# A transformer block's prologue: modulation and k's products ahead of q, q's folds last and in 64 by 64 tiles

## The chip, the core and the metric

The kernel runs on one core of one Trainium2 chip. The metric is the device time of one execution in microseconds. Its engines are TensorE (PE; its weight loads are listed apart as PEld), VectorE (DVE), ScalarE (ACT), GpSimd (POOL) and SyncE (SP), which here only issues transfers. Each engine works through its own list of instructions in order and waits at an instruction until what it needs is there.

## The reference

x has 2048 tokens of 640 features; there are 32 heads of 20. All data are float32.

```python
mod = (silu(c) @ w_mod).reshape(1, 6, 1, 640)
sa, ca, ga, sb, cb, gb = ...              # six rows of 640
h = layernorm(x) * (1 + ca) + sa
q, k, v = split_heads(h @ wqkv)
pq = einsum("bhsd,hdf->bhsf", q, w_phi)   # the same for pk
phi = concat([softmax(p), softmax(-p)])   # of pq and of pk
kv = einsum("bhsf,bhsd->bhfd", phi_k, v); z = phi_k.sum over tokens
o = (phi_q @ kv) / (phi_q . z + 1e-6)
x = x + ga * (o @ wo)
h = layernorm(x) * (1 + cb) + sb
x = x + gb * (relu(h @ w1 + b1)**2 @ w2 + b2)
```

## The kernel before

**Tiling.** Tokens go in 16 tiles of 128, features in 5 chunks of 128. x is loaded, normalised and transposed two token tiles at a time (a pair; pair 0 holds tiles 0 and 1). A matrix is held as a high part in a rounded format and a low part, the rest; a product is three matmuls: high by high, high by low, low by high (`three`, L87). ScalarE copies the high part, VectorE subtracts to get the low part (`lo`, L90).

**Folding.** w_phi is multiplied into the q and k columns of wqkv, so that a projection gives pq or pk at once. `fold` (L265) does this for one chunk d of 128 features: the raw columns, transposed on the host, are the stationary operand and a block-diagonal tile of w_phi (`bd_t`, six heads to a block of 120) is the moving one; five matmuls of 120 columns and one of 40 fill two PSUM tiles, each float32 matmul as two instructions. `split` then makes the high and the low part.

**Modulation.** `mod_rows2` (L568) multiplies silu(c) with one chunk of the first two modulation rows in four column groups; `mod_sb` copies the sums, `mod_cols2` transposes them and reduces them on VectorE to one column of scale and shift per chunk. `t_in` transposes normalised x, `t_out` applies that column on ScalarE (`hf`, then the high part `hT`) and VectorE subtracts the low part. `stats` takes the mean and variance of a pair on VectorE and finishes them on GpSimd; `scale` normalises in place on ScalarE.

**Order.** The prologue up to the values of tiles 0 and 1 is written out by hand: each engine does its instructions in the order in which the code writes them. It opens with `WARM` matmuls on a tile of ones. Behind it, TensorE's order is still by hand, that of the other engines is set by the scheduler of the language from its own estimate of the times. In the prologue before, SyncE issues k, x pair 0, q (four chunks), modulation chunks 0 and 1, q's last, the other modulation chunks, x pair 1, v. TensorE folds all of k and four chunks of q, then does the modulation rows and transposes of x, and k's products (`k_step`, L603: chunk d for tiles 0 and 1, so the two tiles hold all four buffers of the `pj` PSUM tiles). Then come q, x pair 1's transposes, q of tile 1, v of tiles 0 and 1, and from there tile by tile k, v and q, with the products of phi_k and v (`do_kv`, L443, tile `kvp`) for two tiles at a time. These need the exponentials of both tiles divided by their sums (`k_norm`, L437). `spread` subtracts maximum and minimum per head, `exps` takes the exponentials.

Of the kernel before, what the change touches and what calls it, by code (L numbers as in the profile page):

```python
# [26 lines left out]
NG = len(GR)  # L27
NU = 11
# [7 lines left out]
WARM = 9  # L36
# [18 lines left out]
def kernel(  # L55
# [8 lines left out]
    bd: bass.AP,  # L64
    c: bass.AP,
# [98 lines left out]
    make_identity(nc, ident)  # L164
    neg = const.tile([P, P], F32R, name="neg")
# [36 lines left out]
    nc.scalar.dma_start(c_t, c)  # L202
    bd_t = row("s4", "bd_t")
    raw, WM, RV, XB = {}, {}, {}, {}

    def load_raw(nm, w5, w1, ds=range(NC)):
        if 0 in ds:
            raw[nm] = [tok2("w", f"raw_{nm}{i}") for i in range(3)]
            nc.vector.memset(raw[nm][2][:, 1], 0.0)
        for d in ds:  # L210
            nc.sync.dma_start(raw[nm][d // 2][:, d % 2], w5[d * P : (d + 1) * P])
            if d == 0:
                nc.sync.dma_start(raw[nm][2][:40, 1], w1)
# [5 lines left out]
    def load_wm(d):  # L219
        WM[d] = flat(tok2(("k", "k", "q0", "q1", "w")[d], f"wm_{d}"))  # L220
        nc.sync.dma_start(WM[d], w_ss[d * P : (d + 1) * P])
# [4 lines left out]
    load_raw("k", wk5, wk1)  # L226
    load_x(0)
    load_raw("q", wq5, wq1, range(4))
    for d in range(2):
        load_wm(d)  # L230
    load_raw("q", wq5, wq1, (4,))
    for d in range(2, NC):
        load_wm(d)
    load_x(1)
    for d in range(NC):
# [3 lines left out]
        nc.sync.dma_start(RV[d], wv[d * P : (d + 1) * P])  # L239
# [25 lines left out]
    def fold(nm, d, p=None):  # L265
# [4 lines left out]
        for g, (o, n) in enumerate(GR):  # L270
            if g < 5:
                r = raw[nm][d // 2][:120, d % 2, g * P : (g + 1) * P]
            else:
                r = raw[nm][2][:120, 1, d * P : (d + 1) * P]
            nc.tensor.matmul(  # L275
                p[g // 3][:, (g % 3) * 120 : (g % 3) * 120 + n], r, bd_t[:120, g * 120 : g * 120 + n],
                start=True, stop=True,
            )

        def split():  # L280
            for h, (a, b) in enumerate(((0, 360), (360, 640))):
# [261 lines left out]
    def stats(xt, nm):  # L543
# [5 lines left out]
        for i in range(2):  # L549
            for h in range(2):  # L550
                nc.vector.bn_stats(st[:, i, h], xt[:, i, h * HALF : (h + 1) * HALF])
            nc.vector.bn_aggr(mv[:, i], st[:, i])
        nc.gpsimd.tensor_scalar(sq, mv[:, :, 1], EPS, None, op0=ALU.add)
# [3 lines left out]
        return nb, sq  # L557
# [10 lines left out]
    def mod_rows2(*ds):  # L568

        p = tp(f"mrow{ds[0]}")  # L570
        for m, d in enumerate(ds):
# [45 lines left out]
    for d in range(4):  # L617
        fold("k", d)()
# [1170 lines left out]
```

## Time and profile before

| | us |
|---|---|
| median of 3 runs (lowest, highest) | 747.8 (746.73, 747.94) |
| the profiled execution | 746.64 |
| its span, first to last instruction | 744.9 |
| TensorE / VectorE / ScalarE / GpSimd busy | 738.1 / 598.8 / 453.1 / 169.1 |

The profiled execution takes 1.74 us outside its span. A row of a timeline gives the start, the duration, the engine, the line of the kernel, the operation, out<-in, the shape and the count of instructions merged into it, and in brackets the idle time before them with what ended it. Times are from the start of the span. In a row of the chain of waits the line is that of a helper where one records the matmul (L81). TensorE's ends are modelled, its starts are recorded. A row of a table of windows gives the stretch, its length, and each engine's busy time with its count of instructions, then TensorE's granted clock, the share of busy transfer engines and GB/s.

### The profile page before, as it was taken

To read this page: it belongs to the slowest core of one execution; us is meant where nothing else is said; L and a number is where in the kernel's file an instruction comes from. 1 tells how busy PE (TensorE), PEld (TensorE's weight loads), DVE (VectorE), ACT (ScalarE), POOL (GpSimd) and SP (SyncE) were. 2 spreads that over 40 slices of the span, in tenths; PEclk is the share of its full clock that TensorE was granted. 3 is DMA by queue.
4 is the path that set the end of the run, shared out by engine and by line. 5 is a ranking of instruction groups with operands and counts; after the bars stand their busy time and mean duration, and the time that the engine had idled before them with its cause. 6 is when DMAs were issued, how large, how long until landed. Compare 5 with 4: busy or idle time off the path is not lost.

```text
span 744.9 us, 16612 instructions
## 1 busy us (share of the span) xinstructions
PE 738.1 (99%) x6523; PEld 720.6 (97%) x6523; DVE 598.8 (80%) x1089; ACT 453.1 (61%) x1028; POOL 169.1 (23%) x352
## 2 busy tenths in 40 slices
PE   9999999999999999999999999999999999999997
PEld 9999999999999988998999999999999999999997
DVE  6598988987999999999755777877786776777766
ACT  5767566657863355567687667475574747647431
POOL 2000101001100337547303040231321313222110
PEclk9999999999999999999999999999999999999999
DMA  8812341343331254754885567897667768667461
GB/s 330 339 37 106 111 134 59 107 143 107 126 124 72 83 184 152 173 137 106 209 251 166 154 199 255 271 312 211 180 190 201 214 184 240 187 176 213 129 183 36
DMA packets 58800, 126.46 MB, mean 170 GB/s; under 512 B 7438, under 2 KB 16403, under 8 KB 58723
## 3 DMA queue, kind: packets, MB, share of 16 engines
q1 hardware_dynamic: 38636, 79.20, 32.4%
q0 software_dynamic: 17504, 40.90, 22.1%
q10 hardware_dynamic: 2583, 5.30, 1.9%
q8 instruction: 51, 0.84, 0.5%
q14 instruction: 26, 0.21, 0.1%
HBM read 100.74 MB, written 29.89 MB: 175 GB/s over the span
## 4 chain that ended last, share of the span: by engine, by line
PE 88%; DVE 6%; ACT 3%; POOL 1%; issue 1%; ACTq 0%; DVEq 0%; POOLq 0%
PE up L81 25%; PE acc L81 18%; PE pk L81 8%; PE pwo L81 8%; PE pv L81 8%; PE pq L81 6%; PE acc3x L81 5%; PE te L943 2%; PE kvp L448 1%; DVE dn L875 1%; PE foldk L275 1%; PE numa L81 1%; PE ta L357 1%; DVE scr L873 1%; PE foldq L275 1%
## 5 line engine op out<-in xcount | busy, mean ns | idle before, releaser
L81 PE MATMUL up<-h,w 128*128 128x256 f32 x1640 | 204.6, 276 | 0.1
L81 PEld LDWEIGHTS up<-h,w 128*128 128x128 f32 x1640 | 196.5, 188 | 0.7 <-DVE h L91 0.5
L1338 ACT ACTIVATE ft<-up,b_t 128x256 f32<-128x256 f32 x104 | 49.2, 473 | 95.6 <-PE up L81 95.2
L81 PE MATMUL acc<-w,ra 128*128 128x384 f32 x452 | 97.5, 335 | 0.0
L1339 DVE TENSOR_TENSOR ft<-ft 128x256 f32<-128x256 f32 x104 | 43.8, 421 | 43.0 <-ACT ft L1338 41.5
L81 PE MATMUL pwo<-wo,ot 128*128 128x384 f32 (+1 forms) x480 | 78.1, 313 | 0.0
L81 PE MATMUL pq<-wq,hT 128*128 128x384 f32 (+1 forms) x480 | 75.8, 312 | 0.0
L81 PEld LDWEIGHTS acc<-w,ra 128*128 128x128 f32 x452 | 72.7, 188 | 0.8 <-DVE ra L91 0.6
L81 PE MATMUL pk<-wk,hT 128*128 128x384 f32 (+1 forms) x480 | 73.1, 309 | 0.0
L81 PE MATMUL pv<-wv,hT 128*128 128x380 f32 (+1 forms) x480 | 73.0, 309 | 0.0
L81 PEld LDWEIGHTS pwo<-wo,ot 128*128 128x128 f32 x480 | 69.5, 188 | 2.8 <-issue 2.7
L81 PEld LDWEIGHTS pq<-wq,hT 128*128 128x128 f32 x480 | 71.3, 188 | 0.7 <-issue 0.5
L81 PEld LDWEIGHTS pv<-wv,hT 128*128 128x128 f32 x480 | 71.3, 188 | 0.0
L81 PEld LDWEIGHTS pk<-wk,hT 128*128 128x128 f32 x480 | 70.8, 188 | 0.5 <-ACT hT L369 0.2
L91 DVE TENSOR_TENSOR ra<-ft,ra 128x384 fp32r<-128x384 f32 (+2 forms) x86 | 36.8, 448 | 32.6 <-ACT ra L1362 18.8
L1448 POOL DMA_DIRECT2D ring_a<-td_a x34 | 18.5, 543 | 117.2 <-PE acc L81 103.5
L1362 ACT ACTIVATE ra<-ft 128x384 fp32r<-128x384 f32 x48 | 25.2, 526 | 28.4 <-DVE ft L1339 22.3
L81 PE MATMUL acc3x<-w,ra 128*128 128x256 f32 x231 | 39.5, 278 | 0.0
L81 PEld LDWEIGHTS acc3x<-w,ra 128*128 128x128 f32 x231 | 37.2, 188 | 0.0
L439 DVE TENSOR_REDUCE sk<-ek 128x64 f32<-128x1280 f32 x16 | 23.7, 1482 | 15.1 <-ACT ek L434 10.7
L1353 DVE TENSOR_TENSOR ft<-ft 128x128 f32<-128x128 f32 x136 | 33.3, 286 | 1.2
L334 POOL TENSOR_SCALAR sma<-sma 128x2 f32<-128x2 f32 x6 | 3.1, 516 | 134.9 <-ACT xb L333 134.9
(255 smaller groups left out, 1442.5 us busy)
## 6 DMA issues: line engine op xcount, KB each, us to landing
ring_c<-td_c POOLq DMA_DIRECT2D x34, 384.0 KB, 4.0
ring_a<-td_a POOLq DMA_DIRECT2D x34, 384.0 KB, 3.4
ring_b<-td_b POOLq DMA_DIRECT2D x34, 256.0 KB, 3.6
esp<-eq SPq DMA_DIRECT2D x12, 640.0 KB
el<-esp SPq DMA_DIRECT2D x12, 640.0 KB
rw<-in_w SPq DMA_DIRECT2D x23, 320.0 KB
wm<-in_w_mod SPq DMA_DIRECT2D x20, 320.0 KB
xb<-in_x SPq DMA_DIRECT2D x8, 640.0 KB
```

The source lines that it names most:

```text
L81: nc.tensor.matmul(o, a, b, start=first and i == 0, stop=last and i == len(terms) - 1, skip_group_check=skip,)
L91: (eng or nc.vector).tensor_tensor(out_lo, full, hi.bitcast(F32), op=ALU.subtract)
L275: nc.tensor.matmul(p[g // 3][:, (g % 3) * 120 : (g % 3) * 120 + n], r, bd_t[:120, g * 120 : g * 120 + n], start=True, stop=True,)
L357: nc.tensor.transpose(p[:, i * P : (i + 1) * P], src, ident)
L439: nc.vector.tensor_reduce(s, heads(flat(e)), axis=AX.X, op=ALU.add)
L448: nc.tensor.matmul(kvp[0][32 * c : 32 * c + DH + 1, a - g % 3 * DH : a - g % 3 * DH + 2 * m].rearrange("p (s n) -> p s n", s=2)[:, :, h % ...
L943: nc.tensor.transpose(p[:124, a : a + P], EU[2 * j + i][:, 2 * g + c, :124], ident)
L1338: nc.scalar.activation(r, p, AF.Relu, bias=b1_t[:, f : f + 1])
L1339: nc.vector.tensor_tensor(r, r, r, op=ALU.mult)
L1353: nc.vector.tensor_tensor(t[:, o], t[:, a], t[:, b], op=op)
L1362: nc.scalar.activation(a[:, 0, :3], t[:, :3], AF.Copy)
L1448: nc.gpsimd.dma_start(RING[j, n, r], TD[n][r].bitcast(F32R))
```

## The change

**Loads.** SyncE issues k chunks 0 and 1, x pair 0, k chunks 2 and 3, modulation chunk 0, k chunk 4, modulation chunks 1 to 3, x pair 1, modulation chunk 4 and then q. v's loads are put after the code of the prologue's k products. A one-element copy on GpSimd from q's chunk 3 into v's first tile holds them until that chunk has landed; in SyncE's list they come behind five loads for the gate modulation, which use the memory of the five copied modulation rows.

**TensorE's order.** Only four k folds come first, then modulation chunk 0, x's transposes and k's last fold; k's products begin at once, with the transpose of the next modulation column between the two tiles of a step and the modulation rows of the one after behind it. q's folds come last, chunk 0 before k's last step, the others behind it.

**q's folds.** q's raw columns are laid out anew: heads 0 to 15 on partitions 0 to 59, heads 16 to 31 on 64 to 123. The new tile `bq_t` holds three heads to a block of 60. A group of columns is four matmuls of 64 by 64 by 60, one for each half of the rows and of the columns; the two row halves write to two PSUM tiles, which are now four fixed ones in turn (`kvp` 1 with the one of `tp`, `kvp` 2 with `kvp` 0). A chunk has 24 matmuls (48 instructions) in place of 6 (12), with half the depth.

**The rest.** Two warm matmuls less; x pair 1's statistics are split around chunk 0's q fold; k's results of tile 1 are copied behind all q copies, x pair 1's scaling after them, then v's high parts; tile 1's `spread` follows all of v's low parts.

```diff
-WARM = 9
+WARM = 7
...
+    own6 = bdc[:, 376:382]
+    own_q = own6[:, :3]
...
+    nc.scalar.dma_start(bdc[:, 256:376], bdq)
+    bq_t = row("s4", "bq_t")
...
+    for step in ("k0", "k1", "x0", "k2", "k3", "m0", "k4", "m1", "m2", "m3", "x1", "m4", "q0", "q1", "q2", "q3", "q4"):
...
+    def load_v():
+        nc.gpsimd.tensor_copy(RV[0][:1, :1], raw["q"][1][:1, 1, :1])
+        for d in range(NC):
+            nc.sync.dma_start(RV[d], wv[d * P : (d + 1) * P])
...
+        if nm == "q":
+            for g, (o, n) in enumerate(Q_FOLDS):
+                r = raw[nm][d // 2][:, d % 2, g * P : (g + 1) * P] if g < 5 else raw[nm][2][:, 1, d * P : (d + 1) * P]
+                for a in (0, 64):
+                    for c in (0, 64):
+                        nc.tensor.matmul(
+                            p[a // 64][c : c + 64, o : o + n], r[a : a + 64, c : c + 64], bq_t[a : a + 64, o : o + n],
+                            start=(g == 0), stop=True, skip_group_check=True,
+                        )
...
-    for d in range(4):
+    for d in range(2):
         fold("k", d)()
-    n0 = stats(XB[0], "a0")
-    fold("k", 4)()
-    fold("q", 0, kvp[1:])()
-    fold("q", 1)()
+    _, n0 = stats_parts(XB[0], "a0")
+    nc.vector.tensor_tensor(
+        bq_t[:, :360].rearrange("p (g i f) -> p g i f", i=3, f=DH),
...
+    for d in range(2, 4):
+        fold("k", d)()
     scale(XB[0], *n0)
-    fold("q", 2)()
-    split = fold("q", 3)
     mod_rows2(0)
     mod_sb(0)
     for d in range(NC):
         t_in(XB[0], d, TR[d])
-    split()
+    fold("k", 4)()
     mod_cols2(0)
     out0(0)
     mod_rows2(1)
     mod_sb(1)
...
+    def fold_q(d):
+        p = (kvp[2], kvp[0]) if d % 2 else (kvp[1], tp(f"foldq{d}"))
+        fold("q", d, p)()
...
+    for d in range(NC):
+        k_step(d, lambda: next_out(d + 1))
+        if d + 2 < NC:
+            mod_rows2(d + 2)
+            mod_sb(d + 2)
+        if d == 2:
+            next(n1)
+        if d == 3:
+            fold_q(0)
+            n1 = next(n1)
+    load_v()
     load_x(2)
...
+    to_sb(PP[0], PK[0])
+    for d in range(1, NC):
+        fold_q(d)
+    to_sb(PP[1], PK[1])
+    scale(XB[1], *n1)
...
-    for d in range(1, NC):
+    for d in range(NC):
         v_hi(d)
...
+    v_lo(0)
+    v_lo(1)
     spread(PK[0], EK[0], "k0")
     exps(EK[0])
-    v_lo(1)
     v_lo(2)
-    spread(PK[1], EK[1], "k1")
     v_lo(3)
     v_lo(4)
+    spread(PK[1], EK[1], "k1")
     do_q(0)
```

Three places show how it moves instructions. A row gives the line, the operation, out<-in and the shape; xN merges N alike. Line numbers of the changed kernel are its own (L305 and L295 are the folds, L609 the modulation rows, L389 x's transposes, L622 the modulation's transposes, L83 the products).

TensorE before, from the first modulation rows to k's first product:

```order
L577 MATMUL mrow0_362<-wm_0_151,cs_175 32x128 x10
L357 MATMUL kvp0_76<-ident_87,xb0_140 128x128 x2
L357 MATMUL kvp1_77<-ident_87,xb0_140 128x128 x4
L357 MATMUL kvp2_78<-ident_87,xb0_140 128x128 x4
L590 MATMUL kvp0_76<-ident_87,msb0_373 128x128
L577 MATMUL mrow1_395<-wm_1_153,cs_175 32x128 x10
L275 MATMUL foldq4_0_409<-bd_t_129,raw_q2_144 128x120 x3
L275 MATMUL foldq4_1_410<-bd_t_129,raw_q2_144 128x120 x2
L275 MATMUL foldq4_1_410<-bd_t_129,raw_q2_144 128x40
L590 MATMUL kvp0_76<-ident_87,msb1_406 128x128
L577 MATMUL mrow2_423<-wm_2_156,cs_175 32x128 x10
L81 MATMUL pk0_0_438<-wk0_235,hT0_222 128x384 x3
```

TensorE with the change, at the same place (behind k's fold 3):

```order
L305 MATMUL foldk3_1_291<-bd_t_134,raw_k2_138 128x40
L609 MATMUL kvp0_76<-wm_0_144,cs_177 32x128 x10
L389 MATMUL kvp1_77<-ident_87,xb0_155 128x128 x4
L389 MATMUL kvp2_78<-ident_87,xb0_155 128x128 x4
L389 MATMUL kvp0_76<-ident_87,xb0_155 128x128 x2
L305 MATMUL foldk4_0_327<-bd_t_134,raw_k2_138 128x120 x3
L305 MATMUL foldk4_1_328<-bd_t_134,raw_k2_138 128x120 x2
L305 MATMUL foldk4_1_328<-bd_t_134,raw_k2_138 128x40
L622 MATMUL kvp0_76<-ident_87,msb0_314 128x128
L609 MATMUL kvp0_76<-wm_1_145,cs_177 32x128 x10
L83 MATMUL pk0_0_357<-wk0_235,hT0_224 128x384 x3
```

Two modulation steps and q's chunk 4 stood between x's transposes (L357) and the first product; now x's transposes come ahead of k's last fold, and one modulation step stands before the first product.

ScalarE before, from x pair 1's scaling to v's last high part (`wv0` to `wv4` are v's high parts, `k0` and `k1` the copies of k's results of tiles 0 and 1):

```order
L561 ACTIVATE xb1_162<-xb1_162,nba1_504,sqa1_503 128x640 x2
L658 ACTIVATE wv0_565<-rawv0_164 128x640
L424 ACTIVATE k0_568<-pk0_0_438 128x384
L424 ACTIVATE k0_568<-pk0_1_439 128x256
L424 ACTIVATE k1_571<-pk1_0_440 128x384
L424 ACTIVATE k1_571<-pk1_1_441 128x256
L658 ACTIVATE wv1_574<-rawv0_164 128x640
L658 ACTIVATE wv2_576<-rawv2_167 128x640
L658 ACTIVATE wv3_578<-rawv2_167 128x640
L658 ACTIVATE wv4_580<-rawv4_170 128x640
```

ScalarE with the change, from q's last copies to the same end:

```order
L314 ACTIVATE wq4_626<-kvp1_77 128x320
L314 ACTIVATE wq4_626<-foldq4_625 128x320
L456 ACTIVATE k1_534<-pk1_0_359 128x384
L456 ACTIVATE k1_534<-pk1_1_360 128x256
L595 ACTIVATE xb1_164<-xb1_164,nba1_454,sqa1_453 128x640 x2
L705 ACTIVATE wv0_659<-rawv0_149 128x640
L705 ACTIVATE wv1_661<-rawv0_149 128x640
L705 ACTIVATE wv2_663<-rawv2_150 128x640
L705 ACTIVATE wv3_665<-rawv2_150 128x640
L705 ACTIVATE wv4_667<-rawv4_151 128x640
```

Scaling and v's first high part stood ahead of the copies of k's results; now they stand behind all of q's copies and the last of k's.

VectorE before, around the division of k tile 3 (`ek3` divided by `sk3`; behind the prologue, where the scheduler sets the order):

```order
L439 TENSOR_REDUCE sk3_1121<-ek3_1100 128x64
L91 TENSOR_TENSOR hT2_1008<-hfa2_4_1148,hT2_1008 128x256
L428 TENSOR_REDUCE mxq3_1168<-q3_1164 128x32
L429 TENSOR_REDUCE mxq3_1168<-q3_1164 128x32
L440 RECIPROCAL sk3_1121<-sk3_1121 128x64
L431 TENSOR_TENSOR eq3_1167<-q3_1164,mxq3_1168 128x640 x2
L441 TENSOR_TENSOR ek3_1100<-ek3_1100,sk3_1121 128x1280
L428 TENSOR_REDUCE mxk4_1335<-k4_1188 128x32
L429 TENSOR_REDUCE mxk4_1335<-k4_1188 128x32
L476 TENSOR_REDUCE rs_q_106<-eq3_1167 128x64
L291 SCALAR_TENSOR_TENSOR wm1280_3_1177<-wm1280_3_1177,cs_175,wm1280_2_1026 128x640
```

VectorE with the change, at the same place:

```order
L93 TENSOR_TENSOR hT2_1096<-hfa2_4_1236,hT2_1096 128x256
L460 TENSOR_REDUCE mxq3_1256<-q3_1252 128x32
L461 TENSOR_REDUCE mxq3_1256<-q3_1252 128x32
L471 TENSOR_REDUCE sk3_1209<-ek3_1188 128x64
L463 TENSOR_TENSOR eq3_1255<-q3_1252,mxq3_1256 128x640 x2
L460 TENSOR_REDUCE mxk4_1423<-k4_1276 128x32
L461 TENSOR_REDUCE mxk4_1423<-k4_1276 128x32
L472 RECIPROCAL sk3_1209<-sk3_1209 128x64
L508 TENSOR_REDUCE rs_q_110<-eq3_1255 128x64
L323 SCALAR_TENSOR_TENSOR wm1280_3_1265<-wm1280_3_1265,cs_177,wm1280_2_1114 128x640
L473 TENSOR_TENSOR ek3_1188<-ek3_1188,sk3_1209 128x1280
```

The division now follows the two reductions of `k4`, the sum `rs_q` and the modulation step `wm1280_3`, which all came after it, while `hT2` chunk 4 and q3's reductions went ahead of the sum `sk3`.

153 lines of the change are left out of this document (82 added, 71 removed).

## The prediction

> **What bounds the kernel now.** I read the page's totals first, then the chain of waits in order of time for the first 80 us, then the timeline of each engine there.
>
> ```profile
> span 744.9 us, 16612 instructions
> PE 738.1 (99%) x6523; PEld 720.6 (97%) x6523; DVE 598.8 (80%) x1089; ACT 453.1 (61%) x1028; POOL 169.1 (23%) x352
> 1.05 4.21 PE warm L616 x18
> 5.26 6.80 PE foldk L275 x60
> 12.06 1.34 PE kvp L275 x12
> 13.40 4.02 PE foldq L275 x36
> 17.41 0.78 PE mrow L577 x20
> 18.19 1.24 PE kvp L357 x10
> 24.63 0.11 PE kvp L590
> 28.32 5.20 PE pk L81 x36
> 33.52 4.31 PE pq L81 x30
> 43.22 8.81 PE pv L81 x60
> 52.03 4.34 PE pk L81 x30
> 60.77 1.41 PE kvp L448 x125
> ...
> 5.26:33.52 28.26, 28.26 (x296) 26.96 (x296) 16.61 (x46) 19.55 (x45) 3.29 (x10) 1.00 1.03 393
> ```
>
> The chain rows give start, duration, engine, result and line. TensorE carries the chain from 1.05 us on, and in the window from its first fold to q's first product (33.52) it is busy in all 28.26 us. The prologue is therefore a sum of TensorE work, with folds of both matrices (1.34 us a chunk) put where the loads, x's statistics and the modulation are being waited for. Whatever leaves TensorE there is gained; whatever makes it wait there is lost. The rest of the program follows at a TensorE that hardly ever waits, so a shift at 60 us is still there at the end. The second thing to see is VectorE behind it:
>
> ```profile
> 32.82 0.82 DVE L91 TENSOR_TENSOR wv<-rawv,wv 128x640 fp32r<-128x640 f32 x1 [1.89 <-ACT wv L658]
> 55.63 1.48 DVE L441 TENSOR_TENSOR ek<-ek,sk 128x1280 f32<-128x1280 f32 x1
> 86.38 1.49 DVE L441 TENSOR_TENSOR ek<-ek,sk 128x1280 f32<-128x1280 f32 x1
> ...
> 32.82:87.86 55.04, 50.39 (x66) 1.00 0.25 85
> ...
> 89.74 1.48 PE L448 MATMUL kvp<-ek,vt 128*21 128x40 f32 x128
> ```
>
> From v's first low part (32.82) to the division of k tile 3 (86.38, ends 87.87) it is busy 50.39 of 55.04 us. The division of tile 1 ends at 57.11, 3.7 us before the kv products that need it (60.77); that of tile 3 ends 1.9 us before its kv products (89.74). These two margins are what a late VectorE can use up.
>
> **The start.** Two warm matmuls less are worth 2 x 4.21/9 = 0.94 us of TensorE, but the first fold stands behind the block-diagonal tile as well:
>
> ```profile
> 4.25 0.85 DVE L243 TENSOR_TENSOR bd_t<-bdc 120x360 f32<-120x360 f32 x2 [1.99 <-DMA bdc<-in_bd]
> 5.05 7.00 PE L275 MATMUL foldk<-bd_t,raw_k 120*128 120x120 f32 x60
> ```
>
> Its first part is made at 4.25 to 4.78, so the fold can start 0.2 us earlier at most. I take nothing. The extra transfer of q's diagonal and the five small GpSimd instructions lie beside this and cost nothing, since what they make is first needed by an instruction behind x's statistics; late, they would cost what they are late.
>
> **The loads.** When they land is read from SyncE's issues, which wait for the transfer eight places earlier:
>
> ```profile
> 8.07 1.15 SPq L221 DMA_DIRECT2D wm<-in_w_ss  x2
> 8.89 0.33 SPq L221 DMA_DIRECT2D wm<-in_w_ss  x1
> 10.83 0.33 SPq L211 DMA_DIRECT2D raw_q<-in_wq  x1
> ...
> SPq L211 <- DMA xb<-in_x: 1.6, 1, 1.6
> SPq L221 <- DMA raw_k<-in_wk: 0.8, 2, 0.5
> ```
>
> They say that k chunk 3 had landed by 8.07, chunk 4 by 8.89, x by 10.83, which is after 1.4, 1.7 and 2.4 MB. With the same bytes in the new sequence, x lands at about 8.1, k chunk 2 at 8.9, chunk 3 at 9.9, the first modulation chunk at 11.7 (0.65 MB more at the 0.393 MB per us of the window above), k chunk 4 at 12.5. TensorE then does k's chunks 0 and 1 from 5.05 to 7.9, waits 1.0, does 2 and 3 from 8.9 to 11.6 and the first modulation rows to 12.5. q's loads land at some 21 to 25, before their use at 29. v's are queued behind five loads that wait for the last modulation transpose (28 us by the sum below); they land by 35 and are used at 39, so holding them costs nothing (of the one-element copy that holds them, GpSimd has nothing behind it until the next tiles' statistics). Without that cover ScalarE would stop there, and behind v's copies q's results with it.
>
> **From x to the first product.** Statistics come behind the low part of chunk 1 in VectorE's order:
>
> ```profile
> 6.63 0.99 DVE L91 TENSOR_TENSOR wk<-foldk,wk 128x360 fp32r<-128x360 f32 x2 [0.73 <-ACT wk L282]
> 7.97 0.99 DVE L91 TENSOR_TENSOR wk<-foldk,wk 128x360 fp32r<-128x360 f32 x2 [0.35 <-ACT wk L282]
> 11.55 0.88 DVE L551 BATCH_NORM_STATS2 sta<-xb 128x6 f32<-128x320 f32 x2
> 13.46 0.21 DVE L552 BATCH_NORM_AGGREGATE mva<-sta 128x2 f32<-128x12 f32 x1
> 15.43 1.73 ACT L561 ACTIVATE xb<-xb,nba,sqa 128x640 f32<-128x640 f32 x2 [0.25 <-POOL nba L556]
> 19.81 0.15 DVE L592 TENSOR_REDUCE cols_a<-kvp 128x2 f32<-128x4 f32 x1
> 20.60 0.42 ACT L369 ACTIVATE hT<-hfa 128x256 fp32r<-128x256 f32 x1
> ```
>
> They start at 8.96 instead of 11.55; 2.12 us later they are done (11.08), scaling starts 1.76 after that (12.84) and ends at 14.57. The ten transposes wait for it: TensorE stands 2.1 us from 12.5, transposes to 15.87, and only then has chunk 4's fold (to 17.21). Its low part ends 2.57 after the fold's start (5.05 to 7.62 for chunk 0), at 18.44, and the first modulation column is reduced behind it on VectorE. From the reduction to the transposed, modulated x took 19.81 to 21.02, so k's first product is at **19.75**: another 1.6 us of waiting, the second modulation rows (0.78) inside it. It was at 22.7. This is where I chose: all waits are charged in full since the order has nothing else for TensorE there.
>
> A step of k is 5.20/3 = 1.73, one transpose 0.11 and one set of rows 0.78 between: 2.62. That covers the path from a transpose to the next chunk (24.63 to 26.18 now). Three such steps, one of 1.84, a q fold and the last 1.73 end k's products at 19.75 + 7.86 + 1.84 + 0.85 + 1.73 = 32.0.
>
> **The q folds.** No instruction of before works on 64 by 64 tiles. Nearest are those that use a part of the columns or of the rows:
>
> ```profile
> 247.92 0.87 PE L811 MATMUL z<-kvs,ident 21*128 21x360 f32 x8
> ```
>
> z, on four row groups: 1280 columns at two half passes. A fold has 640 columns x 2 passes in 1.34 us, 1.05 ns each, so z is worth 2.7 us alone and took 0.87: 3 at a time. The kv products give the other bound, 11 ns per instruction (1.41 us for 125, of 40 columns in four column groups). A q chunk is 48 instructions of mostly 60 columns: 48 x 11 = 0.53 at the least; 320 columns x 4 x 2 x 1.05 = 2.7 us if nothing runs side by side; 0.9 at z's three. I take 0.85, next to z, which has row groups and a bank for each as the q fold has. Each fold then saves 0.49, 2.4 in all. The Trainium skill, "TensorE: Matmul & The Clock Gate", section "Wait — 56ns, not 53.3ns?", has a floor of about 25 ns from one matmul's start to the next, which would make a chunk 1.2 us and the five 1.75 us longer than in my sum. The kv row, 11 ns, does not agree with it.
>
> ```profile
> 18.51 0.76 ACT L282 ACTIVATE wq<-foldq 128x360 fp32r<-128x360 f32 x2
> 32.70 1.39 ACT L424 ACTIVATE k<-pk 128x384 f32<-128x384 f32 x4
> ```
>
> Folds 1 to 4 stand between k's and q's products with two sets of banks, where before they filled waits. Copies of a chunk take 0.76 (the like pair of q's copies), the second low part ends about 0.5 later: fold 3 waits for fold 1's low part. 32.0, 32.9, 33.7 | 34.2, 35.05 | 35.9: q's products start at **35.9**, 2.4 us later than the 33.52 of now.
>
> **VectorE behind it.** ScalarE's order has all q copies (36.7), two of k's copies (0.70, half of 1.39: 37.4), x tile pair 1's scaling (1.74: 39.1) and then v's first high part (0.7). VectorE's first low part of v starts at 39.8, not 32.82: **7.0 late**, with k's first tile ready since 32 and waiting behind it. From there it has its 50.39 us up to the division of tile 3; the order now also puts ahead of this division four instructions that came after it (k4's two reductions, a sum, a modulation step):
>
> ```profile
> 65.51 1.49 DVE L439 TENSOR_REDUCE sk<-ek 128x64 f32<-128x1280 f32 x1 [2.38 <-ACT ek L435]
> 87.78 0.81 DVE L428 TENSOR_REDUCE mxk<-k 128x32 f32<-128x640 f32 x1
> 91.42 1.55 DVE L431 TENSOR_TENSOR ek<-k,mxk 128x640 f32<-128x640 f32 x2
> ```
>
> 3.64 us (87.78 to 91.42). One wait for an exponential pair remains, 1.5 of the 2.38. 39.8 + 50.4 + 3.6 + 1.5 = 95.3, and the kv products of tiles 2 and 3 start there instead of at 89.74: **5.6 us later**. On the way, tile 1's division ends at 39.8 + 24.3 = 64.1, 3.4 later than kv's start now, so 3.4 of the 5.6 are lost by then. After it VectorE is ahead of TensorE again (the division of tile 5 now precedes its q work). Nothing behind that gives time back.
>
> The sum against the profiled execution: 746.64 + 5.6 = 752.2. That execution lies 1.2 below the median of the runs shown (747.8, within 746.73 to 747.94), so I add half of that: 752.8.
>
> **Rivals.** (1) VectorE's 1.9 us margin holds and the division of tile 3 isn't late, since part of the 50.39 can run while it waits for ScalarE: then the 3.4 us at tile 1 is all, 750.0 to 751.2. For it: VectorE has 4.65 us idle before 87.86. Against it: the four instructions put ahead of the division.
>
> (2) Faster: the path from x to k's first product overlaps more than I charge. The sum runs on from this product: q's products 16.15 later, tile 1's division 44.35 later. It decides at 16.4 us (60.77 - 44.35), provided tile 3's division is not pushed out either; below 17.4 TensorE alone would be ahead. With the first product at 15, 746.6 - 1.4 = 745.2, or 746.4 from the median. For it: the 5.1 us of waiting in my sum (1.0, 2.1, 1.6 and 0.45 between the q folds) are the whole loss, against 2.4 us of folding saved. Against it: statistics, scaling, transposes, chunk 4 and the reduction follow one another on four engines, each with its row above. Between 16.4 and 17.5 lies no change.
>
> (3) TensorE slower than its rows. Warm instructions take 4.21/18 = 0.234 us, folds 6.80/60 = 0.113: with the shorter warming and the wait at 8 us, the slow pace could reach into k's first two folds: 24 x 0.121 = 2.9 more, 755.7. The Trainium skill, "TensorE: Matmul & The Clock Gate", Part 1, has a clock that is released only after about 3.4 us of activity; by it the shorter warming can give this same 755.7 at most. The granted clock in the window above reads 1.00, and nothing in the trace shows a lower one. Or the tiles do not run side by side: 5 x 1.85 less the 0.45 of waiting that it covers, 761.6.
>
> **How the numbers follow.** Forecast 0.44; rival (1) 0.26; (3) 0.12; (2) 0.09 faster and 0.09 no change. What a measurement here can tell is about 0.2%, 1.5 us. Slower 0.82, same 0.09, faster 0.09. The forecast's own range is 750.5 to 755.5. To hold the time 8 times in 10 it reaches down over (1) to 748.0 and up over the first half of (3) to 757.0.
>
> **What would show it.** In the profile after: k's first product near 19.75, the transposes waiting for scaled x some 2 us; a q fold of 0.85 us (0.53 to 2.7); q's first product near 35.9; v's first low part near 39.8 on VectorE; TensorE waiting for VectorE before the kv products, twice. I am wrong if q's products start before 33.5 or v's first low part before 35, and wrong in the size if neither kv product waits.

## The result, and the profile after

The changed kernel takes 757.89 us (median of 4 runs, 754.19 to 758.35) against 747.87 us (746.73 to 748.56) for the kernel before on the same chip: a ratio of 1.0118, 95% interval 1.0096 to 1.0141 (the quotient of the two medians, 1.0134, lies inside it). Its profiled execution took 757.99 us.

From the page of the changed kernel, its span and totals:

```profile
span 756.0 us, 16975 instructions
PE 741.4 (98%) x6699; PEld 722.3 (96%) x6699; DVE 600.1 (79%) x1090; ACT 452.7 (60%) x1028; POOL 166.1 (22%) x357
```

The span grew by 11.1 us, TensorE's busy time by only 3.3. The rest, 7.8 us, is TensorE waiting. The chain of waits of the changed kernel shows where (start, duration, what):

```profile
5.08 4.86 PE foldk L305 x24
...
10.84 0.81 DVE sta L583 x2
...
14.79 1.74 ACT xb L595 x2
16.58 2.18 PE kvp L389 x9
18.76 1.08 PE foldk L305 x6
...
22.52 1.25 PE pk L83 x6
...
68.29 1.41 PE kvp L480 x125
```

In place of an unbroken row of TensorE work, the chain goes from k's first two folds to x's statistics on VectorE, to its scaling on ScalarE, back to TensorE for the transposes, and on to k's first product at 22.52, where it was at 22.7 before. In the kernel before, all folds of k and of q were done by then; here those of k are, and those of q are not. TensorE's timeline of the changed kernel at the places of the prediction:

```profile
15.77 0.33 PE L389 MATMUL kvp<-ident,xb 128*128 128x128 f32 x1 [2.39 <-ACT xb L595]
16.58 2.18 PE L389 MATMUL kvp<-ident,xb 128*128 128x128 f32 x9 [0.48 <-ACT xb L595]
...
37.92 1.32 PE L295 MATMUL kvp<-bq_t,raw_q 64*64 64x60 f32 x52 [0.35 <-DVE wq L93]
...
40.23 4.58 PE L83 MATMUL pq<-wq,hT 128*128 128x384 f32 x30
...
68.22 1.48 PE L480 MATMUL kvp<-ek,vt 128*21 128x40 f32 x128
...
100.71 0.84 PE L480 MATMUL kvp<-ek,vt 128*21 128x40 f32 x64 [2.62 <-DVE ek L473]
101.48 6.13 PE L83 MATMUL pq<-wq,hT 128*128 128x384 f32 x30
```

q's first product starts at 40.23 (before 33.52 in the chain and 33.36 in the timeline: 6.7 to 6.9 later), the kv products of tiles 0 and 1 (the products of phi_k and v) at 68.3 (60.8 before: 7.5 later), and between those of tile 2 and those of tile 3 TensorE stands 2.62 us for the division on VectorE. Windows of the changed kernel, at its first folds, up to q's first product, and around x's wait (the number behind GpSimd's is the granted clock):

```profile
5.00:9.00 4.00, 3.92 (x18) 3.93 (x19) 1.87 (x8) 0.93 (x3) 1.10 (x8) 1.00 1.03 368
...
5.08:40.23 35.15, 30.66 (x476) 27.86 (x476) 15.72 (x46) 16.35 (x37) 4.04 (x16) 0.95 0.76 271
...
16.00:17.00 1.00, 0.52 (x3) 0.42 (x3) 0.00 (x0) 0.78 (x2) 0.00 (x0) 0.53 1.02 394
17.00:18.00 1.00, 1.00 (x7) 1.00 (x6) 0.00 (x0) 0.00 (x0) 0.00 (x0) 0.50 1.08 420
```

From the first fold to q's first product, 4.49 of 35.15 us are idle, where the kernel before had none in 28.26; and at 17 us, behind the wait for x, the granted clock is 0.50. From 5 to 9 us it reads 1.00, yet only 18 fold instructions were done there in 3.92 us.

### The profile page after: what moved, and what is told of

Its sections match the earlier page's. It is cut to its first block, busy times and chain, and to the rows that moved or that the text cites. A ratio compares the mean times of both kernels' runs of the same rounds, so it can differ in the third digit from the quotient of the medians.

```text
span 756.0 us, 16975 instructions
## 1 busy us (share of the span) xinstructions
PE 741.4 (98%) x6699; PEld 722.3 (96%) x6699; DVE 600.1 (79%) x1090; ACT 452.7 (60%) x1028; POOL 166.1 (22%) x357
## 4 chain that ended last, share of the span: by engine, by line
PE 89%; DVE 5%; ACT 2%; DMA 1%; issue 1%; POOL 1%; SPq 0%; ACTq 0%; DVEq 0%
PE up L83 24%; PE acc L83 18%; PE pk L83 9%; PE pv L83 9%; PE pwo L83 8%; PE pq L83 7%; PE acc3x L83 5%; PE te L986 2%; PE kvp L480 1%; PE numa L83 1%; PE ta L389 1%; DMA xb<-in_x 1%; PE numb L83 1%; DVE dn L918 1%; PE foldk L305 1%
## 5 line engine op out<-in xcount | busy, mean ns | idle before, releaser
L83 PE MATMUL up<-h,w 128*128 128x256 f32 x1640 | 204.7, 276 | 0.1
L83 PEld LDWEIGHTS up<-h,w 128*128 128x128 f32 x1640 | 196.5, 188 | 0.7 <-DVE h L93 0.5
L83 PE MATMUL acc<-w,ra 128*128 128x384 f32 x452 | 97.5, 335 | 0.0
L83 PE MATMUL pwo<-wo,ot 128*128 128x384 f32 (+1 forms) x480 | 78.5, 314 | 0.0
L83 PE MATMUL pq<-wq,hT 128*128 128x384 f32 (+1 forms) x480 | 77.5, 316 | 0.0
L83 PE MATMUL pk<-wk,hT 128*128 128x384 f32 (+1 forms) x480 | 74.2, 310 | 0.2 <-ACT hT L401 0.2
L83 PEld LDWEIGHTS acc<-w,ra 128*128 128x128 f32 x452 | 72.7, 188 | 1.0 <-DVE ra L93 0.8
L83 PEld LDWEIGHTS pq<-wq,hT 128*128 128x128 f32 x480 | 72.8, 191 | 0.8 <-issue 0.5
L83 PE MATMUL pv<-wv,hT 128*128 128x380 f32 (+1 forms) x480 | 73.1, 310 | 0.3 <-ACT q L456 0.3
L83 PEld LDWEIGHTS pwo<-wo,ot 128*128 128x128 f32 x480 | 69.9, 188 | 2.8 <-issue 2.7
L83 PEld LDWEIGHTS pk<-wk,hT 128*128 128x128 f32 x480 | 71.2, 188 | 1.3 <-issue 0.6
L83 PEld LDWEIGHTS pv<-wv,hT 128*128 128x128 f32 x480 | 71.3, 188 | 0.5 <-ACT q L456 0.5
L1491 POOL DMA_DIRECT2D ring_a<-td_a x34 | 18.5, 543 | 117.1 <-PE acc L83 103.5
L83 PE MATMUL acc3x<-w,ra 128*128 128x256 f32 x231 | 39.5, 277 | 0.0
L83 PEld LDWEIGHTS acc3x<-w,ra 128*128 128x128 f32 x231 | 37.1, 188 | 0.0
```

The source lines that it names most:

```text
L83: nc.tensor.matmul(o, a, b, start=first and i == 0, stop=last and i == len(terms) - 1, skip_group_check=skip,)
L1491: nc.gpsimd.dma_start(RING[j, n, r], TD[n][r].bitcast(F32R))
```

## The experiments

All times are medians on the same chip as the kernel before; a ratio is to that kernel, with its 95% interval. Its medians in the five groups of runs were 747.87 to 748.82, so a difference between kernels of two groups carries up to 1 us of that.

**Nine warm matmuls in the changed kernel.** There k's first two folds take 4.86 us for 24 instructions, 0.20 each, where those before took 0.113.

```diff
-WARM = 7
+WARM = 9
```

> The changed kernel with nine warm matmuls in place of seven. Theory 'clock': in the changed kernel k's first two folds ran at 0.20 us an instruction (4.86 us for 24) where the kernel before has 0.113, and the first product came at 22.5 instead of 19.75; with nine the first folds run at the fast pace from about 5.3, statistics start near 9, and the kernel is 1.8 to 3 us faster than the changed one (755 to 756, by the profile). Rival 'loads': the first folds were slow because they wait for their chunks; then nothing moves (757 to 758.5).

Measured: 755.2 us (754.49 to 756.03), ratio 1.009 (1.0073 to 1.0108), 2.7 below the changed kernel (2.1 by the ratios, whose intervals overlap; the trace is the firmer evidence). TensorE's timeline with nine:

```profile
5.20 2.87 PE L305 MATMUL foldk<-bd_t,raw_k 120*128 120x120 f32 x24
9.64 2.84 PE L305 MATMUL foldk<-bd_t,raw_k 120*128 120x120 f32 x24 [1.57 <-DMA raw_k<-in_wk]
...
13.92 0.33 PE L389 MATMUL kvp<-ident,xb 128*128 128x128 f32 x1 [0.66 <-ACT xb L595]
14.73 1.20 PE L389 MATMUL kvp<-ident,xb 128*128 128x128 f32 x9 [0.48 <-ACT xb L595]
...
19.29 1.25 PE L83 MATMUL pk<-wk,hT 128*128 128x384 f32 x6 [0.20 <-ACT hT L401]
...
97.57 1.39 PE L480 MATMUL kvp<-ek,vt 128*21 128x40 f32 x64 [2.62 <-DVE ek L473]
```

The first two folds are 2.0 us shorter, the wait for k chunk 2 (forecast: 1.0) appears as 1.57, nine transposes take 1.20 instead of 2.18, and k's first product is at 19.29 instead of 22.52. The pace of the first folds, with what follows from it, was worth 3.2 us there and 2.7 at the end. It does not act through TensorE's own work: k's fold 3 ends at 12.5 to 12.6 in both kernels, since the slow pace only fills the wait for k chunk 2. It acts through VectorE, where x's statistics stand behind the low part of fold 1 and start at 10.8 instead of 8.9; the first transpose of x then starts at 15.77 instead of 13.92, and the half clock behind that longer wait adds the rest. The wait for VectorE at the kv products of tile 3 is the same 2.62.

**Seven warm matmuls in the kernel before.**

```diff
-WARM = 9
+WARM = 7
```

> The kernel before with seven warm matmuls. Theory 'clock': the same slow pace reaches into k's first two folds, 24 instructions x 0.09 = 2.1 us, all of it on the chain: 749.5 to 750. Rival 'loads or order': the slow folds belong to the changed kernel's loads; here two matmuls less gain what the block-diagonal tile lets through, 0 to 0.3 us (747.5).

Measured: 749.9 us (747.6 to 753.29, 10 runs) against 748.28, ratio 1.0028 (1.001 to 1.0047). The profiled execution (span 748.2) does not show the slow pace:

```profile
5.22 6.89 PE L275 MATMUL foldk<-bd_t,raw_k 120*128 120x120 f32 x60 [1.00 <-DVE bd_t L243]
```

60 instructions in 6.89 us are as fast as in the kernel before. So seven warm matmuls do not always lead to slow folds. Of the 3.3 us that this execution takes more than the profiled one of before, 0.3 are there when the kv products near 150 us start; the rest comes from a stop of 1.84 us within them and half clock behind it. The spread of 5.7 us over ten runs fits slow folds that come and go, and it fits that stop as well; no trace of this kernel with slow folds was taken.

**k tile 0's exponentials ahead of v's low parts, in the changed kernel.** It undoes a part of the new order on VectorE.

```diff
+    spread(PK[0], EK[0], "k0")
+    exps(EK[0])
     v_lo(0)
     v_lo(1)
-    spread(PK[0], EK[0], "k0")
-    exps(EK[0])
```

> The changed kernel with VectorE's spread of k tile 0 ahead of v's first two low parts, which now wait behind ScalarE's first copies of v. Behind the prologue the scheduler's order changes with it: the division of k tile 3 again comes before k4's reductions. Theory 'VectorE': its 2.3 us of waiting at 41.7 and the 3.6 us of rows go from the path to the kv products of tiles 2 and 3: the 2.6 us of TensorE's waiting there go, and at most 0.5 elsewhere: 754.5 to 755.5. Rival 'TensorE alone': the wait moves to a later product and the time stays within 1 us of the changed kernel's.

Measured: 755.56 us (754.36 to 757.22), ratio 1.0098 (1.0079 to 1.0117). The kv products of tiles 2 and 3 in this run:

```profile
97.28 1.48 PE L480 MATMUL kvp<-ek,vt 128*21 128x40 f32 x128
```

All 128 run in one piece with no wait, and the median is 2.3 us below the changed kernel (1.5 by the ratios), although k's first folds were slow here too and k's first product came 0.66 later. VectorE's timeline of this run:

```profile
93.58 1.49 DVE L473 TENSOR_TENSOR ek<-ek,sk 128x1280 f32<-128x1280 f32 x1
94.98 0.81 DVE L460 TENSOR_REDUCE mxk<-k 128x32 f32<-128x640 f32 x1
```

Tile 3's division starts at 93.58, in the changed kernel at 99.08. With this edit the order puts it ahead of k tile 4's reductions again, so the two causes, the early exponentials and these reductions out of the way, moved together; the run does not part them.

**Both.**

```diff
-WARM = 7
+WARM = 9
...
+    spread(PK[0], EK[0], "k0")
+    exps(EK[0])
     v_lo(0)
     v_lo(1)
-    spread(PK[0], EK[0], "k0")
-    exps(EK[0])
```

> The changed kernel with both: nine warm matmuls, and k tile 0's exponentials ahead of v's first two low parts. Theory (two losses that add up: the slow pace of the first folds and what follows it, 2.7 us by the run with nine warm matmuls, and TensorE's wait for VectorE before the kv products of tiles 2 and 3, 2.3 us by the run with k tile 0's exponentials first): 757.9 - 5.0 = 752.9, within 752.3 to 753.5, no wait for VectorE before kv(2,3), kv(0,1) at 65 to 66 us. Rival (the two are the same time seen twice: what TensorE gains in front it waits for behind): 754.7 to 755.6.

Measured: 753.15 us (751.73 to 753.52), ratio 1.0056 (1.0034 to 1.0078). The two losses add up: 4.7 us together, 2.7 and 2.3 alone. What is left can be read from its window from the first fold to q's first product:

```profile
5.18:37.22 32.04, 27.44 (x476) 24.57 (x476) 16.18 (x46) 16.41 (x38) 4.06 (x17) 1.00 0.84 301
```

Against 28.26 us without a gap in the kernel before it has 4.60 idle and 0.82 less busy. Five tiled folds save 2.35 of work; the missing 1.5 went into k's steps, 2.84 us each with modulation between the halves where the rows of before give 2.62 (0.9 in four steps), into q's folds 1 to 4 (0.95 each with their waits left out, 0.87 alone: 0.3), and 0.3 I can't place. So 4.60 + 1.5 - 2.35 = 3.8 us at q's first product are the change's own price, with the clock and VectorE out of the way.

**x's waits filled.** As the last kernel, and k chunk 4's fold ahead of x's transposes, q chunk 0's fold behind them, with q's first transfer moved up for it.

```diff
-    for d in range(NC):
-        t_in(XB[0], d, TR[d])
-    fold("k", 4)()
-    mod_cols2(0)
-    out0(0)
+    split_k = fold("k", 4)
+    for d in range(NC):
+        t_in(XB[0], d, TR[d])
+    split_q = fold("q", 0, pj("foldq0"))
+    split_k()
+    mod_cols2(0)
+    out0(0)
+    split_q()
```

> As the kernel with both, and TensorE's waits around x filled: the fold of k's chunk 4 stands ahead of x's transposes, and the fold of q's chunk 0 (loaded behind k's chunk 4) behind them; the copies of both come later. Theory (what is left of the loss is TensorE waiting with nothing in its order): the two folds, 1.34 and 0.87 us, fall into waits, k's first product stays at 19.3 to 19.8 us, 2.2 less than the kernel with both, 750.2 to 751.3. Rival (the copies of the folded chunks delay x's path on ScalarE and VectorE by as much, or q's load delays the modulation): within 0.8 us of the kernel with both.

Measured: 753.84 us (752.78 to 755.31), ratio 1.0075 (1.0049 to 1.0102): no gain over the kernel with both. TensorE's timeline:

```profile
29.89 2.11 PE L83 MATMUL pk<-wk,hT 128*128 128x384 f32 x12 [0.43 <-ACT hT L401]
...
36.50 4.66 PE L83 MATMUL pq<-wq,hT 128*128 128x384 f32 x30
...
155.67 0.92 PE L480 MATMUL kvp<-ek,vt 128*21 128x40 f32 x68 [2.70 <-issue]
```

Of the 2.2 us moved, 0.7 arrive at q's first product (37.22 to 36.50): the steps of k are paced by the path from column to transposed x, which waits again (0.43) where the q fold used to stand. k's first product came 0.58 earlier (18.71), not at the same place. A stop of 2.70 us much later, with no engine named, took more than that in the profiled execution. The theory falls in its size: a third of the moved folds arrives.

**q folded as before, in the changed order.** q's groups of 120 columns, 12 matmul instructions a chunk.

```diff
-        if nm == "q":
-            for g, (o, n) in enumerate(Q_FOLDS):
...
+        if True:
...
-    wq5, wq1 = by_half(A_wqkv[:, :D])
+    wq5, wq1 = by_chunk(A_wqkv[:, :D])
```

> The changed kernel with q folded as before, 12 matmuls of 120 columns a chunk; order, loads and warm matmuls as changed. Theory (each tiled fold saves 0.47 us of TensorE, and those between k's and q's products stand on its path): 5 x 0.47 = 2.35, less 0.35 that folds 2 and 3 wait for copies anyway: 759.4 to 760.4. Rival (there the copies on ScalarE and VectorE set the pace, so the tiles bring nothing): 757.4 to 758.6.

Measured: 760.26 us (757.68 to 762.37), ratio 1.0153 (1.0122 to 1.0184). TensorE at q's first product:

```profile
41.15 4.62 PE L83 MATMUL pq<-wq,hT 128*128 128x384 f32 x30
```

Against 40.23 in the changed kernel, with k's first product 0.32 earlier: the tiles save 1.2 us in the profile and 2.4 by the medians, whose intervals overlap. By the profile they help in this order; the medians alone do not show it.

**v's loads not held.**

```diff
-        nc.gpsimd.tensor_copy(RV[0][:1, :1], raw["q"][1][:1, 1, :1])
...
+    load_v()
+
     by_head = bdc[:120, :120]
...
-    load_v()
     load_x(2)
```

> The changed kernel with v's loads not held: they stand right behind q's in SyncE's order and start when their buffers come free. Theory (the hold costs nothing but the 0.24 us that one copy waits for its load): 757.0 to 758.3. Rival 1 (the hold makes VectorE's first low part of v late): 755.5 to 756.5, first low part before 43 us. Rival 2 (v's loads push q's loads out, as the hold is there to avoid): over 759, a q fold waiting for its load.

Measured: 758.16 us (753.07 to 761.68), ratio 1.0121 (1.0074 to 1.0169): no difference from the changed kernel that four runs can tell. The trace has two, and they go opposite ways. k's first folds ran at the fast pace, though with seven warm matmuls, and the stop is in q's last fold:

```profile
19.98 1.25 PE L83 MATMUL pk<-wk,hT 128*128 128x384 f32 x6 [0.20 <-ACT hT L402]
...
39.09 0.26 PE L296 MATMUL foldq<-bq_t,raw_q 64*64 64x60 f32 x1 [1.81 <-issue]
...
39.65 5.76 PE L83 MATMUL pq<-wq,hT 128*128 128x384 f32 x30
```

k's first product is 2.5 us earlier than in the changed kernel. Then TensorE stops 1.81 us in the middle of a fold, and the products behind the stop take 5.76 us instead of 4.58, so that q's first product is only 0.6 earlier. No data and no engine is late at the stop ("issue" is time in which the engine waited for nothing that the profile shows). The equal medians are therefore not yet proof that the hold costs nothing. The next kernels are about such stops.

**Only the tiles, in the order before.** Loads and order as before, nine warm matmuls, all of q in tiles.

```diff
+        if nm == "q":
+            for g, (o, n) in enumerate(Q_FOLDS):
...
-    wq5, wq1 = by_chunk(A_wqkv[:, :D])
+    wq5, wq1 = by_half(A_wqkv[:, :D])
```

> The kernel before in its own order, with q's folds alone as 64 by 64 tiles (an extra diagonal tile is built on VectorE between k's folds 1 and 2). Theory 'tiles good, order bad': the folds take 0.87 us as in the changed kernel against 1.34, 2.3 us less TensorE work; ScalarE's copies pace them at 1.0, so 1.0 to 2.2 us faster than before (745.6 to 746.8). Rival 'tiles bad': switching between tile shapes or the copies take the gain back; 747.5 to 749.

Measured: 754.09 us (751.61 to 754.79), ratio 1.0071 (1.005 to 1.0092), where theory and rival both had it close to the kernel before. TensorE's timeline:

```profile
13.88 1.71 PE L292 MATMUL foldq<-bq_t,raw_q 64*64 64x60 f32 x94 [0.45 <-DMA raw_q<-in_wq]
18.53 1.61 PE L292 MATMUL foldq<-bq_t,raw_q 64*64 64x20 f32 x50 [2.94 <-issue]
...
24.84 0.54 PE L292 MATMUL foldq<-bq_t,raw_q 64*64 64x60 f32 x23 [0.34 <-issue]
```

After 46 of the 48 matmul instructions of chunk 2's fold TensorE stops for 2.94 us, and once more in chunk 4's. The transfers of the same run in the window of the first stop (queue, kind, packets, MB, share of the 16 engines):

```profile
q1 hardware_dynamic: 316, 1.14, 98.3%
q8 instruction: 1, 0.02, 2.3%
```

One packet of instructions moved in it, among loads that fill the transfer engines. The windows of the same run say how many matmul instructions had run at each stop, and what the clock did behind the first:

```profile
0.00:18.52 18.52, 13.74 (x220) 13.29 (x220) 11.77 (x30) 9.58 (x20) 5.95 (x37) 1.00 0.89 313
0.00:24.83 24.83, 19.71 (x346) 18.25 (x346) 13.68 (x35) 12.28 (x27) 5.95 (x37) 0.93 0.93 337
...
18.50:22.00 3.50, 3.47 (x73) 2.96 (x74) 0.49 (x1) 0.82 (x3) 0.00 (x0) 0.53 1.03 420
```

220 and 346, 126 apart; and a clock of 0.53 for 3.5 us. q's first product starts at 37.06, 3.7 later than before; a stop of 3.34 us in the kv products near 156 us, whose cause is not known, takes a large part of the rest.

**The same with 24 more matmul instructions in front.**

```diff
-WARM = 9
+WARM = 7
...
+    for i in range(14):
+        nc.tensor.matmul(warm[:, :8], ones, ones[:, :8], start=True, stop=True)
```

> The kernel with only q's tiles added to the old order, with 24 matmuls more ahead of it in TensorE's program: seven warm matmuls and fourteen of 8 columns instead of nine warm ones (28 short records for 4 long). In the run with nine, TensorE stood 2.94 us between the 46th and the 47th of the 48 matmuls of q chunk 2's fold. Theory (it stands there for its own instructions, which come in pieces of a fixed size behind the loads, and short matmuls use a piece up sooner than the next one comes): the stop moves by as many matmuls, to about the 22nd of the same fold. Rival (it waits for q's data or for a buffer, which the profile does not name): it stays at the 46th, or at the start of a fold.

Measured: one run of 749.8 us. The short warm matmuls took longer than expected (3.29 us for 28), so that the folds began at 7.34 instead of 5.08, and at half clock. TensorE's timeline, and its window up to the one stop that is left:

```profile
23.56 0.26 PE L292 MATMUL foldq<-bq_t,raw_q 64*64 64x60 f32 x1
24.89 0.89 PE L292 MATMUL foldq<-bq_t,raw_q 64*64 64x60 f32 x47 [1.06 <-issue]
```

```profile
0.00:24.88 24.88, 22.08 (x346) 20.75 (x346) 13.55 (x35) 12.12 (x27) 5.92 (x37) 0.93 0.93 338
```

The second stop moved from the 25th to the 1st instruction of chunk 4's fold, by exactly the 24 that were added, and stands at the same count, 346. A wait for data or a buffer would have stayed at its place in the program. With one run the time itself proves nothing; the place of the stop does. The first stop, expected at the 22nd of chunk 2's fold, is gone: there TensorE came some 2.7 us later than in the run before, which would give the next piece time to arrive. Together with the packet in the window of the stop, this is the theory's mechanism: TensorE waits for its own instructions.

**The old sequence of loads in the changed kernel.**

```diff
-    for step in ("k0", "k1", "x0", "k2", "k3", "m0", "k4", "m1", "m2", "m3", "x1", "m4", "q0", "q1", "q2", "q3", "q4"):
+    for step in ("k0", "k1", "k2", "k3", "k4", "x0", "q0", "q1", "q2", "q3", "m0", "m1", "q4", "m2", "m3", "m4", "x1"):
```

> The changed kernel with the transfers in the old sequence (k, x, q's first four chunks, then the modulation, x's second pair last); v's loads still held, TensorE's order, folds and warm matmuls as changed. Theory (in the new order k's first product hangs on x and the first modulation chunk, so a later load is paid in full, and TensorE, idle for longer, falls back to half clock): the transposes start near 18 us, k's first product at 24 to 25 us instead of 22.5, 759 to 762. Rival (the waits in the new order are set by the chain behind the loads, not by when they land): 757 to 758.6.

Measured: 760.98 us (759.89 to 763.49), ratio 1.0172 (1.0154 to 1.0191). TensorE's timeline:

```profile
17.18 1.49 PE L609 MATMUL kvp<-wm,cs 128*32 128x128 f32 x20 [4.22 <-DMA wm<-in_w_ss]
18.61 2.10 PE L389 MATMUL kvp<-ident,xb 128*128 128x128 f32 x10
...
24.07 1.26 PE L83 MATMUL pk<-wk,hT 128*128 128x384 f32 x6 [0.20 <-ACT hT L401]
```

One wait of 4.22 for the first modulation chunk stands in place of those of 2.39 and 0.48 for x, with the instructions behind it at the slow pace (1.49 instead of 0.85). k's first product is 1.55 later than in the changed kernel, q's 1.84 (42.07). Of the change's parts, the new sequence of loads is what the new order needs: it is worth 3.1 us in it by the medians.

**Two chunks in tiles, in the order before.** Only chunks 3 and 4, whose folds stand apart. In a first run the 20 rows of head 15 in these two chunks were those of head 30; the second has them right. The instructions are the same.

```diff
+TILED = (3, 4)
...
+        if nm == "q" and d in TILED:
```

> The kernel before with the folds of q's chunks 3 and 4 alone in tiles, the order and the warm matmuls of before. Theory (tiles lose in the old order only where three folds of them follow one another; two that stand apart save 0.47 us each, and what follows them can wait for x or the modulation): no stop inside a fold, 0 to 0.9 us below the kernel before on the same chip, 747.0 to 748.2. Rival (what follows is not ready earlier, and the added instructions cost where they are fetched): 0 to 2 us above the kernel before.

> The kernel before with the folds of q's chunks 3 and 4 in tiles and the last rows of w_q placed for them; otherwise as before. By the run of the same instructions with other rows loaded (ratio 0.998, 0.9966 to 0.9994): 0.3 to 2.5 us below the kernel before on the same chip, one stop of about 0.8 us inside the fold of chunk 4. Rival (that difference was chance): within 0.3 us of the kernel before, or above it.

Measured: 748.05 us (745.83 to 749.3, 12 runs) against 748.82, ratio 0.998 (0.9966 to 0.9994); and with the rows right 747.35 us (745.67 to 749.34, 12 runs) against 748.06, ratio 0.9986 (0.9974 to 0.9998). TensorE's timeline of the second:

```profile
17.20 0.89 PE L291 MATMUL foldq<-bq_t,raw_q 64*64 64x60 f32 x48
...
21.66 0.88 PE L291 MATMUL foldq<-bq_t,raw_q 64*64 64x60 f32 x44 [0.41 <-issue]
```

One stop of 0.41 inside a fold is left. Two of five folds in tiles, in the old order, give 0.7 us below the kernel before, at the edge of what these runs can tell, and it is the fastest version here.

## Why the prediction was right or wrong

**Right: the direction, and its cause.** The slower outcome was forecast from TensorE's waits for x and from VectorE's late start, and both are there. The first product does not come earlier in a way that matters, q's products wait for folds that no longer fill anything, and the kv products of tiles 2 and 3 wait for the division of tile 3.

**Too small by 5.1 us (757.9 against 752.8).** The median lies above the forecast's own range (750.5 to 755.5) and 0.9 above the wider one, which ends at 757.0; the ratio's value, 1.0118 x 747.87 = 756.7, is just inside that. The step that failed is the start: k's chunks 0 and 1 "from 5.05 to 7.9". They took to 9.94, at 0.20 us an instruction. The forecast had this pace as rival 3 and kept it out of the sum, "2.9 more". With nine warm matmuls the median is 2.7 lower, but that the two numbers are alike is luck: the folds themselves are 2.0 longer, and that delays x's statistics by 1.8. What the rival and the forecast both missed is a second slow stretch, after the wait for x: nine transposes in 2.18 instead of 1.20. At 22.52 instead of 19.75, k's first product was 2.8 late; with nine warm matmuls it was at 19.29. Up to there the sum holds once the pace is right, in part by luck too: its waits of 1.0, 2.1 and 1.6 for k chunk 2, x and the modulation column measure 1.57, 1.14 and 1.11.

**The k steps.** A step was priced at 2.62 us, with products at 1.73 for twelve. With its products split in sixes a step takes 2.84; from the first product to q's first product the sum had 16.15, and the changed kernel took 17.71 (40.23 - 22.52), the run with both repairs 17.93. That term was 1.6 short.

**The q folds.** 0.85 for a fold was forecast: the trace has 0.89 for the 48 in the kernel with two tiled chunks. The floor of about 25 ns from one matmul's start to the next, which the prediction took from the Trainium skill, "TensorE: Matmul & The Clock Gate", section "Wait — 56ns, not 53.3ns?", does not hold for these tiles: 0.89 / 48 = 18.5 ns each. Fold 3 waited for fold 1's low part, 0.35 us, as forecast (0.45).

**VectorE.** v's first low part was forecast 3.9 us behind q's first product and came 3.8 behind it:

```profile
44.02 1.56 DVE L93 TENSOR_TENSOR wv<-rawv,wv 128x640 fp32r<-128x640 f32 x2 [2.33 <-ACT wv L705]
...
99.08 1.49 DVE L473 TENSOR_TENSOR ek<-ek,sk 128x1280 f32<-128x1280 f32 x1
```

From there to the end of tile 3's division (100.57) it took 56.55 us, against 55.5 in the sum. Rival 1 (the margin holds) falls: the division was late by 2.6 us, and VectorE's order is the cause, as undoing a part of it shows; which part of that order, the run does not tell. But only one of the two waits named came: at the kv products of tiles 0 and 1 TensorE was itself 7.5 late and arrived with the division (68.22). The sum charged 3.4 there to VectorE; the loss was TensorE's own.

**v's loads.** "Holding them costs nothing" is not refuted: with the hold ScalarE waits 0.24 us for one of v's loads, and without it the median is the same within its spread, though the two traces began differently. The reason was incomplete: loads that follow q's at once can also delay TensorE's own instructions (1.81 us in that trace, 0.2 to 0.4 at the same place where v is held).

**What the change loses, by the runs.** In its trace 7.5 us at the kv products of tiles 0 and 1, the wait of 2.62 and the 1.55 that the half clock behind it adds (6.13 - 4.58) make 11.7; the kv products of tiles 4 and 5 start 11.8 later than before (130.51 against 118.69). Of the 10.0 us between the medians, 4.7 go away with nine warm matmuls and the exponentials put first (757.89 to 753.15); of the 5.0 left against its own kernel before, 3.8 are there at q's first product: waits for x, for the modulation column and for k chunk 2, and smaller groups of products, against 2.35 of folding saved. The last 1.2 us are not accounted for one by one. Stops with no engine named, in the kv products at 150 to 166 us, are 0.9 in the profile of the kernel before and between none and 3.3 in the others; they were not tested, and before the longest two (3.34 and 2.70) no packet of TensorE's instructions moved in the 8 us before TensorE went on, so they need not be of the kind of those in the folds.

## What to carry to other kernels

Work that looks like an expense in front of a late input may be the cover of its wait: before it is moved back, ask what TensorE does in its place, and count the stretch at half clock that follows a gap. Warm matmuls that only just suffice are not spare: with two fewer, k's first folds were slow in four of six traces. Splitting a matmul into many short ones saves TensorE's time only while its instructions arrive as fast as it uses them, so short ones are best spread among long ones, above all while loads fill the transfer engines.

## What the runs showed of the hardware

**The clock falls back after gaps from about 1.8 us on.** In these traces the granted clock fell to 0.50 for about 3 us or longer behind each gap of TensorE of 1.81 us or more (1.81, 1.84, 2.01, 2.39 to 2.40, 2.62 to 2.63, 2.70, 2.94, 3.34, 4.22 us) and stayed at 1.00 behind each of 1.0 to 1.57. Between them there are two: 1.75 us, with 0.40 more one transpose later, was followed by 0.50 (q folded as before, 16 us), and 1.76 was not (nine warm matmuls, 195 us). A gap costs more than itself: the products behind the wait of 2.62, 6.13 us in the row at 101.48, take 4.58 where the clock is full (40.23). The Trainium skill, "TensorE: Matmul & The Clock Gate", Part 1, gives an idle window of about 3.4 us that runs free of the kernel; all but one of the gaps here were shorter than that. Being busy is not enough either: behind 28 warm matmuls of 8 columns, with no gap, the clock read 0.50 from 8 to 11 us (the kernel with 24 more instructions in front).

**The slow start does not show in the clock.** In the first folds of the changed kernel the clock reads 1.00 though an instruction took 0.20 us instead of 0.12, so the slow start must be read from durations. From 5 to 9 us, 18 or 19 fold instructions started in four of the six traces with seven warm matmuls and nothing else in front, 24 or more in the other two and in all seven with nine. What decides in a single execution is open.

**Instructions arrive in pieces of 126 matmuls.** In the runs with tiles, stops with nothing waited for stood at 217 to 220, 346 and 471 to 473 matmul instructions from the start, in ten of the kernels, wherever in the program that was:

```profile
0.00:39.08 39.08, 30.69 (x472) 27.42 (x473) 17.82 (x49) 18.04 (x40) 7.42 (x41) 1.00 0.89 320
```

This is v's loads not held; the run with both repairs has its stop of 0.34 us at 472 too, the one with two tiled chunks at 217. One matmul instruction has one weight load, so a piece is some 252 instructions and a few more for waits; the packets of the instruction queue are 0.02 MB, and the page of the kernel before counts 51 of them for 6523 matmuls (6523 / 126 = 51.8). The Trainium skill, "Runtime: NRT & Kernel Launch", Instruction fetch mechanics, has blocks of 16 KiB, 256 instructions, and calls the crossing mostly hidden. The size agrees. The crossing was hidden in the kernel before's prologue, where a fold instruction takes 0.113 us; it cost up to 2.94 us where one takes 0.018 and the loads fill the transfer engines.

**What the loads delay is the packet.** In all eleven of these stops TensorE went on 2.35 to 2.7 us after a packet of its instruction queue had started to move (16.11 and 18.53 with only the tiles). The traces differ in when that packet starts. With v's loads held, it starts 0.7 to 0.9 us after the 346th matmul instruction, in six traces. Without the hold, in one trace, it starts 2.5 after it (36.68 against 34.19), once the loads in front of it are through; from 34 to 36 us they fill the engines:

```profile
q1 hardware_dynamic: 353, 0.79, 100.3%
```
